# Smaller blocks, DMA transposes from tile 8 on, and a new load order in a fused chunk-attention and gated-FFN kernel

## The chip, the cores and the metric

One core of one Trainium2 chip runs the whole program. The metric is device time in microseconds (us), lower is better. The kernel before takes 240.97 us, the median of three runs that lie between 240.74 and 241.13.

## The reference

Chunked attention with memory tokens feeds a gated feed-forward network. There are 4 batches, 8 heads, 768 positions and 64 values per head. Each chunk of 32 queries sees 16 positions to its left, itself, 8 positions to its right, and 8 memory tokens.

```python
for c in range(S // 32):
    l_start, r_end = max(0, 32*c - 16), min(S, 32*c + 32 + 8)
    k_full = concatenate([mem_k, k[:, :, l_start:r_end]], axis=2)
    v_full = concatenate([mem_v, v[:, :, l_start:r_end]], axis=2)
    s = q[:, :, 32*c:32*c+32] @ k_full.T / sqrt(64)
    a = exp(s - max(s)); a = a / (sum(a) + 1e-9)
    out[:, :, 32*c:32*c+32] = a @ v_full
x = out.transpose(0, 2, 1, 3).reshape(3072, 512)
y = (relu(x @ w_gate) * (x @ w_val)) @ w_out       # 512 -> 1536 -> 512
```

Inputs and output are float32.

## The kernel before

**Tiles and blocks.** The 3072 token rows are cut into 24 tiles of 128 rows, 6 to a batch. Attention works tile by tile; the feed-forward network works on blocks of 2 or 4 consecutive tiles (`BLOCKS`, line 51). In a block, each of 12 hidden slices `m` takes four gate matmuls (`g_ps`) and four value matmuls (`v_ps`), both at line 408, as wide as the block (256 or 512 columns). ScalarE (ACT) applies the ReLU (line 414), VectorE (DVE) multiplies the two (line 420). Then each tile of the block takes 12 matmuls of 512 columns against `w_out` (line 433, `out_ps`), ACT copies the result out of PSUM and issues the store.

**Attention of one tile `a`.** Keys and queries are loaded by GpSimd's software DMA queue (POOL, `load_qk`, line 257) with a cast to bf16. Both have to be transposed. For tiles 6 to 10 TensorE (PE) does it (`qk_t`, line 279, 4 matmuls for k and 4 for q, then two copies out of PSUM). From tile `LATE_QK = 11` on, one transposing DMA issued by SyncE (SP) does both (`qk_transfer`, line 283); only the k half is then copied into `kT` (`qk_copy`). Tiles 0 to 5 come in pairs through line 238. The scores are line 310 on PE, followed by max, subtract, sum, reciprocal and normalise on DVE and the exponent on ACT. The probabilities P are transposed on PE for tiles below `LATE_P = 10` (line 359, 4 matmuls and a copy) and by a transposing DMA on SP from then on (line 363). The product with the values is line 389 (`xT_ps`, 16 matmuls; lines 375 and 382 for batch 0), and its copy into the block's `xT` starts the feed-forward matmuls of that block once all its tiles are there.

**Values.** For batches 1 to 3 the value rows are loaded by POOL straight into a zeroed block-diagonal tile `v_bd` (line 184, two large transfers `vl` and two small ones `ve` per batch). The upper context rows are then shifted into place by copies on ACT and DVE (`upper`, called `up` below; 8 for the first half of a batch's tiles and 8 for the second). The rows of the memory tokens (`mem_rows`, line 167, 8 transfers, called `mr`) go through SP for batch 1 and through POOL for batches 2 and 3.

**What sets the order.** Nothing is reordered on the chip: each engine runs its instructions in program order, waiting where an input is missing. The program order comes from a planner in the kernel (`schedule()`), which walks through time with estimated durations and lets each engine take the ready operation of best priority. Attention comes ahead of feed-forward matmuls, which fill what is left of PE. POOL's loads do not go through priorities; they are issued in the order in which they are listed, at most 8 in flight. The planner's estimates for a DMA's landing (`queue_end`, `LAND`, `LAND_P`) decide how far behind a transfer its users are placed in the order.

```python
late = [(a, i) for a in range(TPB, NT) for i in (1, 0)]     # k, q of tiles 6..23
...
for a, i in late[:5]: load_qk_op(a, i)                      # tiles 6, 7 and k of 8
for i in range(2): load(("wo", i), ...)                     # w_out
for b in range(1, B): ...                                   # values, memory rows, q and k by batch
```

Names used below: `vl 1` are the two big value transfers of batch 1, `t8` is the transposing transfer of tile 8's q and k, `pc8` that of its P.

Of the kernel before, what the change touches and what calls it, by code (L numbers as in the profile page):

```python
# [19 lines left out]
def kernel(  # L20
# [27 lines left out]
    KW = CH + NMEM  # L48
    CTX = 16 + CH + 8
    NSET = 2  # L50
    BLOCKS = [2, 2, 2, 4, 4, 4, 4, 2]
    GROUPS = [(0, 2), (2, 6), (6, 9), (9, 12)]
    BAND0 = 48
    UT = 3

    LATE_QK, LATE_P = 11, 10

    KEY_RUNS = ((0, CH, 0), (KW, 64, CH), (CH, KW, CTX))
    assert sum(BLOCKS) == NT and NMEM == 8 and D == 64 and H == 8
# [455 lines left out]


    ISSUE, SLACK = 1.5, 1.0
    LAND = {a: 4.0 if a < 16 else 3.5 if a < 19 else 2.0 for a in range(NT)}
    LAND_P = {a: 3.0 if a < 14 else 2.5 if a < 18 else 2.0 for a in range(NT)}

    def pace_t(a):
        return [("s", a - 5)]
# [136 lines left out]
    load_v_nat(5)  # L659
    for par in range(2):  # L660
        load(("vm", par), 256, 0.3, lambda par=par: mem_values(par))
    for a, i in late[:5]:
        load_qk_op(a, i)
    for i in range(2):
        load(("wo", i), 768, 4.1, lambda i=i: load_out(i))
    for b in range(1, B):
        deps = ([("z0", hp, c0) for hp in range(HP) for c0 in range(0, NCH, 8)] if b > 1 else [("z1", hp) for hp in range(HP)]) + ([("v", TPB * (b - NSET + 1) - 1)] + ['hold'] if b > NSET else [])
        if b == 1:
            for n in range(2 * HP):
                op(("mr", b, n), {"SP": 0.72}, lambda e, b=b, n=n: mem_rows(nc.sync, b, n),  # L670
                   deps + [(("vm", 0), 0.2), (("vm", 1), 0.2)], (0,))
        for par in range(2):
            load_v_op(b, par, deps)
        if b == 2:
            for n in range(2 * HP):
                load(("mr", 2, n), 192, 0.22, lambda n=n: mem_rows(nc.gpsimd, 2, n),
                     deps + [(("vm", 0), 0.2), (("vm", 1), 0.2)])
        for a, i in late[(5, 20, 26)[b - 1]:(20, 26, 36)[b - 1]]:
            load_qk_op(a, i)
    for n in range(2 * HP):  # L680
        load(("mr", 3, n), 192, 0.22, lambda n=n: mem_rows(nc.gpsimd, 3, n),
             deps + [(("vm", 0), 0.2), (("vm", 1), 0.2)])

    op("hold", {"DVE": 0.1}, lambda e: nc.vector.memset(v_bd[1][0:2 * CH, 0, 0, :].bitcast(F32), 0.0), [("v", 2 * TPB - 1)],  # L684
       prio=(0,), after=[("tc",17,1)])
# [6 lines left out]
    def schedule():  # L692
        done, started, times = {}, set(), [0.7]
        free = {e: 0.7 for e in ("PE", "ACT", "DVE", "SP", "POOL")}
        queue_end, flying, gives = 0.0, [], [(WARM + 0.15, "fps")]
        room["fps"] -= 1
        heapq.heappush(times, WARM + 0.15)
        todo = {e: [] for e in free}
        order, n_load = [], 0
        names = lambda o: [d[0] if timed(d) else d for d in o["deps"]] + o["after"]  # L700
        missing = {k: len(set(names(o))) for k, o in ops.items()}
        users = {}
        for k, o in ops.items():
            for d in set(names(o)):
                users.setdefault(d, []).append(k)

        def offer(k):
            for e in ops[k]["eng"]:
                bisect.insort(todo[e], (ops[k]["prio"], k), key=lambda x: x[0])

        for k in ops:
            if not missing[k]:
                offer(k)

        def ready(o, t, margin=0.0):
            if any(d not in started for d in o["after"]):
                return False
            for d in o["deps"]:
                d, lag = d if timed(d) else (d, 0.0)
                if d not in done or done[d] + lag + margin > t + 1e-9:  # L720
                    return False
            return all(room[r] >= o["take"].count(r) for r in o["take"])

        while len(started) < len(ops) + len(loads):
            t = heapq.heappop(times)
            while times and times[0] <= t + 1e-9:
                heapq.heappop(times)
            for g in [g for g in gives if g[0] <= t + 1e-9]:
                gives.remove(g)
                room[g[1]] += 1  # L730
            flying = [f for f in flying if f > t]
            moved = True
            while moved:
                moved = False
                for e in ("POOL", "PE", "ACT", "DVE", "SP"):
                    if free[e] > t + 1e-9:
                        continue
                    if e == "POOL":
                        if n_load == len(loads):
                            continue  # L740
                        o = loads[n_load]
                        if len(flying) >= 8 or not ready(o, t):
                            continue
                        n_load += 1
                        key = o["key"]
                        if o["n"]:
                            end = t + 0.62 + 0.27e-3 * o["n"]
                            queue_end = max(queue_end, end + 0.8) + o["work"]
                            flying.append(queue_end + 1.0)
                            done[key] = queue_end + (1.2 if n_load < 8 else 4.5 if key[:2] == ("vl", 1) else 2.4 if n_load < 45 else 6.0 if key[0] == "vl" else 4.0)  # L750
                        else:
                            end = done[key] = t + max(o["work"], 0.6)
                        fn = o["fn"]
                    else:
                        o = None
                        soon = False
                        for _, key in todo[e]:
                            late_pe = e == "PE" and t > 36.0 and ops[key]["prio"][0] == 1
                            if ready(ops[key], t, MARGIN if late_pe else 0.0):
                                o = None if soon and key[0] in ("up", "z0") else ops[key]  # L760
                                break
                            soon = soon or ready(ops[key], t + 0.3)
                        if o is None:
                            if e == "PE" and 1.3 < t < WARM:
                                order.append((t, lambda: idle_product(256)))
                                free[e] = t + (0.213 if t < 9.0 else 0.11)
                                heapq.heappush(times, free[e])
                            elif e == "PE" and t <= 1.3:
                                heapq.heappush(times, 1.31)
                            continue  # L770
                        for x in o["eng"]:
                            todo[x].remove((o["prio"], key))
                        d = o["eng"][e]
                        d, lat = d if isinstance(d, tuple) else (d, d)
                        d *= (1.8 if e == "PE" and t < 8.0 and key[0] in ("t", "p", "sh", "f") else 1.0)
                        end = t + d
                        done[key] = end + 0.25 if e == "PE" else t + lat + 0.08

                        if e == "SP" and key[0] in ("t", "pc"):
                            queue_end = max(queue_end, t + 1.5) + {"t": 2.6, "pc": 1.3}[key[0]]  # L780
                            done[key] = queue_end + 1.0
                        elif queue_end > t and key[0] == "oc":
                            queue_end += 0.7
                        fn = lambda o=o, e=e: o["fn"](e)
                        for g in o["give"]:
                            g, lag = g if isinstance(g, tuple) else (g, 0.0)
                            gives.append((done[key] + lag, g))
                            heapq.heappush(times, done[key] + lag)
                    for r in o["take"]:
                        room[r] -= 1  # L790
                    started.add(key)
                    for k in users.get(key, ()):
                        missing[k] -= 1
                        if not missing[k]:
                            offer(k)
                    order.append((t, fn))
                    free[e] = end
                    lags = {d[1] for k in users.get(key, ()) for d in ops[k]["deps"] if timed(d) and d[0] == key}
                    for x in [end] + [done[key] + lag + m for lag in lags | {0.0, 0.2, 1.5} for m in (0.0, MARGIN)]:
                        heapq.heappush(times, x)  # L800
                    moved = True
            assert times, [k for k in ops if k not in started][:20]
        return order
# [33 lines left out]
```

## Time and profile before

| | |
|---|---|
| median of three runs | 240.97 us |
| the profiled execution's own time | 240.65 us |
| its span, first to last instruction | 238.9 us (1.75 us lie around it) |
| granted TensorE clock | 0.998 |
| PE busy | 232.5 us, 97% of the span |
| DVE / ACT / POOL busy | 145.3 / 135.5 / 77.4 us |
| DMA moved | 26.88 MB, mean 113 GB/s |
| software DMA queue q0 (POOL) | 76128 packets, 14.65 MB |
| hardware DMA queue q1 (SP: transposes, memory rows) | 23312 packets, 5.53 MB |
| transposing transfers | 13 of q and k, 14 of P |

In the views, PE is the matmul side of TensorE and PEld its weight loads; a busy span of one matmul (about 380 ns at 512 columns) overlaps the next, so the pace is read from the starts of neighbouring groups. "L408" is line 408 of the kernel. Idle time is given in brackets with what ended it.

### The profile page before, as it was taken

How to read it: one execution, taken by the hardware profiler on the slowest of the kernel's cores; microseconds unless marked ns; L12 is line 12 of the kernel's file. 1: busy time of each engine (PE TensorE's matmuls, PEld its weight loads, DVE VectorE, ACT ScalarE, POOL GpSimd, SP SyncE). 2: the span in 40 equal slices, each digit the busy share in tenths (PEclk: the TensorE clock that was granted, in tenths of full speed). 3: DMA queues.
4: the chain of work that ended last, by engine and by line, in shares of the span. 5: the costliest groups of instructions: out<-in, count | busy, mean ns of one | idle time of the engine just before them, and what ended most of it. 6: DMA issues, size and time to landing. Idle time of an engine off the chain costs nothing.

```text
span 238.9 us, 6437 instructions
## 1 busy us (share of the span) xinstructions
PE 232.5 (97%) x2654; PEld 137.7 (58%) x2654; DVE 145.3 (61%) x292; ACT 135.5 (57%) x284; POOL 77.4 (32%) x102
## 2 busy tenths in 40 slices
PE   7898999999999999999999999999999999999994
PEld 5577887785589644455544444444555444445873
DVE  6674876987888389994279851599960043410430
ACT  7577777866885456897566851365523233312422
POOL 8975779313920374700094552100000000000000
PEclk9999999999999999999999999999999999999999
DMA  6999999999999999996199999995121300012102
GB/s 74 171 179 202 201 166 161 206 133 125 190 166 138 131 156 118 122 129 136 70 141 101 135 154 91 113 209 64 27 43 47 127 4 0 0 47 88 44 3 88
DMA packets 103069, 26.88 MB, mean 113 GB/s; under 512 B 94080, under 2 KB 99968, under 8 KB 103040
## 3 DMA queue, kind: packets, MB, share of 16 engines
q0 software_dynamic: 76128, 14.65, 92.7%
q1 hardware_dynamic: 23312, 5.53, 23.2%
q10 hardware_dynamic: 3600, 6.29, 8.4%
q8 instruction: 21, 0.34, 0.7%
q14 instruction: 8, 0.07, 0.2%
HBM read 28.55 MB, written 6.29 MB: 146 GB/s over the span
## 4 chain that ended last, share of the span: by engine, by line
PE 93%; DMA 2%; POOL 2%; issue 1%; ACT 1%; ACTq 0%; POOLq 0%
PE v_ps L408 27%; PE g_ps L408 26%; PE out_ps L433 26%; PE xT_ps L389 3%; PE s_ps L310 2%; DMA v_n<-in_v_dram 2%; PE idle_ps L140 2%; PE vs_ps L216 2%; PE xT_ps L382 2%; PE qk_ps L279 1%; PE pT_ps L359 1%; POOL qk_p L229 1%; PE qk_ps L238 1%; PE xT_ps L375 1%; POOL v_n L200 0%
## 5 line engine op out<-in xcount | busy, mean ns | idle before, releaser
L420 DVE TENSOR_TENSOR gvT<-v_ps,g_relu 128x256 f16<-128x256 f32 (+1 forms) x96 | 53.0, 554 | 48.7 <-PE v_ps L408 35.1
L408 PE MATMUL v_ps<-xT,w_val_sb 128*128 128x256 f16 (+1 forms) x384 | 78.2, 326 | 0.1
L408 PE MATMUL g_ps<-xT,w_gate_sb 128*128 128x256 f16 (+1 forms) x384 | 78.1, 326 | 0.0
L414 ACT ACTIVATE g_relu<-g_ps 128x256 f16<-128x256 f32 (+1 forms) x96 | 47.0, 490 | 41.5 <-PE g_ps L408 39.8
L433 PE MATMUL out_ps<-w_out_sb,gvT 128*128 128x512 f16 (+2 forms) x300 | 65.8, 371 | 0.0
L408 PEld LDWEIGHTS <-w_gate_sb 128*128 128x128 f16 x384 | 36.9, 98 | 24.8
L408 PEld LDWEIGHTS <-w_val_sb 128*128 128x128 f16 x384 | 35.9, 98 | 22.5 <-issue 0.5
L433 PEld LDWEIGHTS <-gvT 128*128 128x128 f16 x300 | 27.6, 97 | 29.5
L79 ACT COPY o_sb<-out_ps 128x512 f32<-128x512 f32 (+2 forms) x25 | 14.2, 568 | 29.6 <-PE out_ps L433 19.4
L323 DVE TENSOR_REDUCE mx<-s_ps 128x8 f32<-128x512 f32 x24 | 16.4, 685 | 13.9 <-PE s_ps L310 13.5
L338 ACT ACTIVATE p_exp<-dif 128x256 f16<-128x256 f32 (+2 forms) x72 | 19.6, 339 | 6.3 <-DVE dif L330 6.1
L184 POOL DMA_DIRECT2D v_bd<-in_v_dram x12 | 11.0, 924 | 33.6 <-DVE v_bd L684 19.2
L342 DVE TENSOR_REDUCE sm<-p_exp 128x8 f32<-128x512 f16 x24 | 16.4, 683 | 5.0 <-ACT p_exp L338 4.8
L257 POOL DMA_DIRECT2D qk_b<-in_k_dram x18 | 16.2, 902 | 9.7 <-DMA v_bd<-in_v_dram 5.4
L257 POOL DMA_DIRECT2D qk_b<-in_q_dram x18 | 16.2, 899 | 9.7 <-DMA v_bd<-in_v_dram 7.2
L79 ACT COPY v_bd<-v_bd 24x768 f16<-24x768 f16 (+1 forms) x23 | 18.5, 823 | 1.2 <-ACT o_sb L79 0.9
L353 DVE TENSOR_TENSOR p_n<-p_exp,rinv 128x512 f16<-128x512 f16 x24 | 16.5, 686 | 0.3
L330 DVE TENSOR_TENSOR dif<-s_ps,mx 128x512 f32<-128x512 f32 x24 | 16.2, 674 | 0.2
L79 ACT CAST xT<-xT_ps 128x512 f16<-128x512 f32 x17 | 10.0, 586 | 8.5 <-PE xT_ps L389 7.3
L167 POOL DMA_DIRECT2D v_bd<-vmem x16 | 10.2, 645 | 12.4 <-DMA qk_b<-in_q_dram 6.1
L140 PE MATMUL idle_ps<-idle 128*128 128x256 bf16 x69 | 11.3, 314 | 1.1 <-DVE warm L477 1.1
L389 PEld LDWEIGHTS <-v_bd 128*128 128x128 f16 x288 | 9.8, 96 | 3.6
(60 smaller groups left out, 165.6 us busy)
## 6 DMA issues: line engine op xcount, KB each, us to landing
out_dram<-o_sb ACTq DMA_DIRECT2D x23, 256.0 KB
qk_b<-in_k_dram POOLq DMA_DIRECT2D x18, 128.0 KB, 8.0
qk_b<-in_q_dram POOLq DMA_DIRECT2D x18, 128.0 KB, 8.9
v_bd<-in_v_dram POOLq DMA_DIRECT2D x6, 384.0 KB, 11.2
w_out_sb<-in_moe_w_out_dram POOLq DMA_DIRECT2D x2, 768.0 KB, 10.5
qk_p<-in_k_dram POOLq DMA_DIRECT2D x3, 256.0 KB, 5.3
qk_p<-in_q_dram POOLq DMA_DIRECT2D x3, 256.0 KB, 6.3
v_n<-in_v_dram POOLq DMA_DIRECT2D x6, 128.0 KB, 6.5
```

Source lines behind the costliest of these rows:

```text
L79: nc.scalar.copy(o, i)
L257: nc.gpsimd.dma_start(qk_b[a][:, 1 - i], bass.AP(tensor=x.tensor, offset=x[b, 0, 128 * t, 0].offset, ap=[[D, 128], [S * D, H], [1, D]]))
L323: nc.vector.reduce_max(SM[a, "mx"], s4, axis=AX.X)
L330: nc.vector.tensor_tensor(out=SM[a, "dif"].rearrange("p (m r) a s -> p r m a s", r=2), in0=S_ps.pop(a).rearrange("p r (m a) s -> p r m a s ...
L338: nc.scalar.activation(p[:, :, :, s0:s0 + k1 - k0], dif[:, :, :, k0:k1], ACT.Exp, scale=SCALE)
L342: nc.vector.reduce_sum(SM[a, "sm"], SM[a, "p"], axis=AX.X)
L353: nc.vector.tensor_tensor(out=P_n[a], in0=SM.pop((a, "p")), in1=rinv_b, op=ALU.mult)
L389: nc.tensor.matmul(ps[:, hp, r], lhsT=v_bd[b % NSET][:, hp, 4 * t + g, :], rhs=x[:, hp, r], start=True, stop=True)
L408: nc.tensor.matmul(ps, lhsT=w[:, f, 128 * m:128 * m + 128], rhs=xTs[blk][:, f, :], start=(f == 0), stop=(f == NFC - 1))
L414: nc.scalar.activation(st["r", m], st.pop((0, m)), ACT.Relu)
L420: nc.vector.tensor_tensor(out=st["gv"][:, m, :], in0=st.pop((1, m)), in1=st.pop(("r", m)), op=ALU.mult)
L433: nc.tensor.matmul(st["o", t, c], lhsT=st["gv"][:, m, 128 * t:128 * t + 128], rhs=w_out_sb[:, m, c[0]:c[1]], start=(m == 0), stop=(m == ND ...
```

## The change

- `BLOCKS` becomes 2, 2, 2, 2, 2, 4, 4, 4, 2: the first block of four (tiles 6 to 9) is cut in two, the rest keep their tiles.
- `LATE_QK` goes from 11 to 8 and `LATE_P` from 10 to 8: q and k of tiles 8, 9 and 10, and P of tiles 8 and 9, are transposed by DMA instead of on PE.
- POOL's list is written as `ORDER`: q and k of tiles 6 to 9 (8 loads), both halves of w_out, the values of batch 1, 10 loads (tiles 10 to 14), values and memory rows of batch 2, 8 loads (tiles 15 to 18), values of batch 3, 10 loads (tiles 19 to 23), memory rows of batch 3. Before, 5 loads stood ahead of w_out, 15 behind the values of batch 1 (to tile 15), and 6 behind batch 2.
- The planner's estimates change: landing margins of 3.0 (q, k) and 2.5 (P) for every tile, smaller margins for late loads, and a model in which transposing transfers run one after the other and each delays the software queue. These move instructions in the program order; they do no work themselves.

```diff
-    BLOCKS = [2, 2, 2, 4, 4, 4, 4, 2]
+    BLOCKS = [2,2,2,2,2,4,4,4,2]
...
-
-    LATE_QK, LATE_P = 11, 10
+    ORDER = [8, 'w0', 'w1', 'v1', 10, 'v2', 'm2', 8, 'v3', 10, 'm3']
+
+    LATE_QK, LATE_P = 8, 8
...
-    LAND = {a: 4.0 if a < 16 else 3.5 if a < 19 else 2.0 for a in range(NT)}
-    LAND_P = {a: 3.0 if a < 14 else 2.5 if a < 18 else 2.0 for a in range(NT)}
+    LAND = {a: 3.0 for a in range(NT)}
+    LAND_P = {a: 2.5 for a in range(NT)}
...
+    def v_deps(b):
+        z = [("z0", hp, c0) for hp in range(HP) for c0 in range(0, NCH, 8)] if b > 1 else [("z1", hp) for hp in range(HP)]
+        return z + ([("v", TPB * (b - NSET + 1) - 1), "hold"] if b > NSET else [])
...
+    n_qk = 0
+    for step in ORDER:
+        if isinstance(step, int):
+            for a, i in late[n_qk:n_qk + step]:
+                load_qk_op(a, i)
+            n_qk += step
+            continue
+        kind, b = step[0], int(step[1])
+        if kind == "w":
+            load(("wo", b), 768, 4.1, lambda b=b: load_out(b))
+        elif kind == "v":
+            for par in range(2):
+                load_v_op(b, par, v_deps(b))
+        else:
             for n in range(2 * HP):
...
+                load(("mr", b, n), 192, 0.22, lambda b=b, n=n: mem_rows(nc.gpsimd, b, n), mem_deps(b))
+    if "m1" not in ORDER:
+        for n in range(2 * HP):
+            op(("mr", 1, n), {"SP": 0.72}, lambda e, n=n: mem_rows(nc.sync, 1, n), mem_deps(1), (0,))
...
-                            done[key] = queue_end + (1.2 if n_load < 8 else 4.5 if key[:2] == ("vl", 1) else 2.4 if n_load < 45 else 6.0 if key[0] == "vl" else 4.0)
+                            done[key] = queue_end + (1.2 if n_load < 8 else 4.5 if key[:2] == ("vl", 1) else 2.4 if n_load < 45 else 3.5 if key[0] == "vl" else 2.5)
...
-                            queue_end = max(queue_end, t + 1.5) + {"t": 2.6, "pc": 1.3}[key[0]]
-                            done[key] = queue_end + 1.0
+                            double = key[0] == "t"
+                            busy = queue_end > t + 1.2
+                            begin = max(t + 1.2 + (3.0 if busy else 0.2), turn)
+                            if queue_end > begin:
+                                turn = begin + (3.8 if double else 2.7)
+                                queue_end += 1.6 if double else 0.9
+                            else:
+                                turn = begin + (1.5 if double else 0.9)
+                            done[key] = turn + 0.3
```

More of the change, by code (lines that the diff above doesn't have):

```diff
@@ L661, with mem_deps @@
         load(("vm", par), 256, 0.3, lambda par=par: mem_values(par))
[L662 to L668, printed above, removed]
-            for n in range(2 * HP):
[L670 to L682, printed above, removed]
+    def v_deps(b):
+        z = [("z0", hp, c0) for hp in range(HP) for c0 in range(0, NCH, 8)] if b > 1 else [("z1", hp) for hp in range(HP)]
+        return z + ([("v", TPB * (b - NSET + 1) - 1), "hold"] if b > NSET else [])
+    def mem_deps(b):
+        return v_deps(b) + [(("vm", 0), 0.2), (("vm", 1), 0.2)]
+    n_qk = 0
[12 more added lines that the diff above has]
+        else:
+            for n in range(2 * HP):
+                load(("mr", b, n), 192, 0.22, lambda b=b, n=n: mem_rows(nc.gpsimd, b, n), mem_deps(b))
+    if "m1" not in ORDER:
+        for n in range(2 * HP):
+            op(("mr", 1, n), {"SP": 0.72}, lambda e, n=n: mem_rows(nc.sync, 1, n), mem_deps(1), (0,))
     op("hold", {"DVE": 0.1}, lambda e: nc.vector.memset(v_bd[1][0:2 * CH, 0, 0, :].bitcast(F32), 0.0), [("v", 2 * TPB - 1)],
@@ L694, in schedule @@
         free = {e: 0.7 for e in ("PE", "ACT", "DVE", "SP", "POOL")}
-        queue_end, flying, gives = 0.0, [], [(WARM + 0.15, "fps")]
+        queue_end, turn, flying, gives = 0.0, 0.0, [], [(WARM + 0.15, "fps")]
         room["fps"] -= 1
```

## The prediction

> **What bounds the kernel now.** I read the page's busy line and its chain first.
>
> ```profile
> PE 232.5 (97%) x2654; PEld 137.7 (58%) x2654; DVE 145.3 (61%) x292; ACT 135.5 (57%) x284; POOL 77.4 (32%) x102
> PE 93%; DMA 2%; POOL 2%; issue 1%; ACT 1%; ACTq 0%; POOLq 0%
> ```
>
> PE sets the time: the chain that ended last runs on it for 93% of the span, and the view of waits gives PE 3.0 us of idle time in all, none of it after 50 us. So only two things can move the time: work taken from or given to PE, and waits that appear where none are now. The price of PE work comes from its timeline, from start to start, because busy spans overlap.
>
> ```profile
> 60.73 0.61 PE L279 MATMUL qk_ps<-ident_b,qk_b 128*128 128x128 bf16 x8
> 61.18 1.46 PE L433 MATMUL out_ps<-w_out_sb,gvT 128*128 128x512 f16 x6
> ...
> 68.56 0.38 PE L359 MATMUL pT_ps<-band,p_n 128*128 128x128 f16 x4
> 68.78 0.60 PE L408 MATMUL v_ps<-xT,w_val_sb 128*128 128x256 f16 x4
> 69.22 0.60 PE L408 MATMUL g_ps<-xT,w_gate_sb 128*128 128x256 f16 x4
> ...
> 157.77 1.03 PE L408 MATMUL g_ps<-xT,w_gate_sb 128*128 128x512 f16 x4
> 158.63 1.03 PE L408 MATMUL v_ps<-xT,w_val_sb 128*128 128x512 f16 x4
> ```
>
> Eight transposes of q, k cost 0.45 us, four of P 0.22, a group of four 256-wide matmuls 0.44, of four 512-wide ones 0.86.
>
> Then the waits that are close to becoming PE's. DVE's timeline near 60 us, and the landing of the second big value transfer of batch 1 (issued at 39.3, its row's maximum is its own):
>
> ```profile
> 58.80 1.30 DVE L81 COPY v_bd<-v_bd 24x768 f16<-24x768 f16 x3 [1.03 <-DMA v_bd<-in_v_dram]
> ...
> 63.79 0.69 DVE L342 TENSOR_REDUCE sm<-p_exp 128x8 f32<-128x512 f16 x1
> 64.39 0.68 DVE L323 TENSOR_REDUCE mx<-s_ps 128x8 f32<-128x512 f32 x1
> 64.99 0.19 DVE L346 RECIPROCAL rinv<-sm 128x8 f32<-128x8 f32 x1
> 65.11 0.69 DVE L330 TENSOR_TENSOR dif<-s_ps,mx 128x512 f32<-128x512 f32 x1
> 65.72 0.68 DVE L353 TENSOR_TENSOR p_n<-p_exp,rinv 128x512 f16<-128x512 f16 x1
> ```
> ```profile
> DMA to landing us min/median/max: 15.0/17.2/19.5
> ```
>
> DVE already waits for this landing (58.78) today; PE does not, because tile 6's value matmuls stand at 62.47. Late in the kernel ACT waits for the transposing transfer of tile 23's q, k, and PE uses it 1.5 us later:
>
> ```profile
> 162.75 0.62 ACT L79 COPY kT<-qk_T 128x512 bf16<-128x512 bf16 x1 [1.49 <-DMA qk_T<-qk_b]
> ```
> ```profile
> 164.25 0.31 PE L310 MATMUL s_ps<-kT,qk_T 64*32 64x64 bf16 x32
> 164.50 1.04 PE L408 MATMUL v_ps<-xT,w_val_sb 128*128 128x512 f16 x4
> 165.37 0.56 PE L389 MATMUL xT_ps<-pT,v_bd 128*128 128x32 f16 x16
> ```
>
> So DMA is the second bound, just behind PE, twice.
>
> **PE work.** The instruction order of the changed kernel has 24 transposes of q, k less (tiles 8 to 10) and 8 of P less. Saved: 3 x 0.45 + 2 x 0.23 = 1.81 us. Cutting tiles 6 to 9 into two blocks turns 24 groups of 512 columns into 48 of 256; with the medians over all groups, 0.863 and 0.437 us, that is 20.98 - 20.71 = 0.27 us more. Net **1.55 us less**, with no other place to go but the end, since PE never idles after 50 us. The chain's head (to 54 us) has the same PE order as before: no change.
>
> **Other engines.** The cut costs ACT 12 x (2 x 386 - 595) ns = 2.1 us and DVE 12 x (2 x 420 - 688) ns = 1.8 us; three q copies and two P copies out of PSUM fall away, some 3 x 0.6 + 2 x 0.5 = 2.8 us. Taken as nothing: between 76 and 80 us DVE is busy 2.39 and ACT 1.54 of 4.00 us. Without that room the 1.1 us left over would be added.
>
> **w_out moves behind three loads.** Three loads landed in 1.65 us (59.22 to 60.87) to 2.6 us (37.33 to 39.91). The second half of w_out landed at 48.7 and is first used at about 55.4, so it comes at 51.3 at the latest. Cost nothing; t8 (below) starts on its queue behind the memory rows, whose packets end at 51.5.
>
> **Values of batch 1, the first pinch.** Their last landing, 58.78, moves by those 1.65 to 2.6 us, and by t8 and t9, which are new here: SP issues them right behind the memory rows (46.4), beside these loads. What a transposing transfer takes from the software queue: while t11 to t14 ran, the last four loads landed between 69.13 and 80.37, 11.2 us for what needs 4 x 0.86 = 3.4, so 1.95 us each. Low end 1.4 (t19 with two P transfers, together its size again, cost nine loads 2.8 us: 133.5 to 144.4 instead of 9 x 0.9). High end 2.7: one P transfer, half as big, stretched the second value load of batch 3 to 6.9 us from 4.2 and 5.0 in batches 2 and 1. Two of them: 2.8 to 5.4, taken 3.9, as q, k transfers are the nearest row. Landing: 63.2 to 66.8, taken 58.78 + 2.1 + 3.9 = 64.8.
>
> A rule speaks on this. The Trainium skill ("DMA: Bandwidth & Descriptors", section "Queues, rings and completion order") says that each DMA engine takes turns between the queues it has work for, packet by packet; a transfer would then cost its neighbour its own packets only, and the row above speaks against that.
>
> What waits: DVE stands at the `up` copies, and behind them in its order are tile 7's sum and normalise, tile 8's max and subtract, tile 6's copy into xT and the next gate product. From landing: three copies 1.0, the five softmax steps 2.6 (63.79 to 66.40), xT 0.6, gate 0.45: 4.7 us. That gate frees the PSUM buffer for the fourth value group of block 2. Its place on PE: 54.1 + 48 x 0.216 (w_out) + 0.22 + 2 x 0.25 + 0.44 puts tile 6's values at 65.6; with their 0.42, four groups of 0.437 and P of tile 7 it is 68.0. Stall 64.8 + 4.7 - 68.0 = **1.5 us**, bounds 0 and 3.5.
>
> **Values of batch 2.** Issue to last landing was 12.0 us (81.35 to 93.32) with one P transfer issued near its end. Now pc9, pc10 and pc11 surround it, and t15 moves behind it with two loads more ahead of t16. One P transfer costs 0.7 to 2.7 us; PE's four PSUM buffers cover about 1.7. Taken 0.5, bounds 0 and 2.0.
>
> **Tile 18's values, the second pinch.** They stood at 165.37 behind tile 22's scores; the new order puts them ahead of these, after five 512-wide groups and two scores: 153.93 - 1.55 + 4.3 + 0.5 = 157.2. They need pc18, which SP issues behind t23. t23 waits for the buffer that tile 18's scores free; those move up three w_out groups, 1.95 + 1.55 = 3.5 us. pc18 landed at 163.1, so 159.6: a stall of 2.4 us, or nothing if the queue drains faster than before (memory rows are issued earlier). Taken **1.5**.
>
> **Sum** on the profiled execution's 240.65: -1.55 + 1.5 + 0.5 + 1.5 = +1.95, 242.6. The median lies 0.32 above that execution, so the prediction is 240.97 + 1.95 = **242.9 us**.
>
> **Rivals.**
> - *The cover holds* (faster). v1 lands at the low end, 63.2, and the later queues drain in time: stalls 0 to 1.0, so 239.4 to 240.5, likeliest 239.9. For it: the removed PE work is certain, and every margin above is within 2 us of holding. Against: the DVE row that waits today. It decides at a landing of about 64.0. Chance 0.28.
> - *Shared packet by packet* (no change). A q, k transfer alone ran its packets in 1.46 us (106.10 to 107.56); two delay v1 by 2.9: landing 63.8, stall 0.5; P transfers cost 0.9 and stay covered; 0.75 at tile 18. Sum -1.55 + 1.25: 240.7. With some friction up to 241.4. Against: 11.2 us for four loads. Chance 0.11. By the skill's rule of turns this would be the case.
> - *Each pinch at its bound* (much slower): 3.5 + 2.0 + 2.4 - 1.55 = +6.35, 247.3. For it: a late load delays the transfers that wait for it, and SP issues in order. Chance 0.12, from 245 up.
> - That the transposes are not gone is excluded by the order of the changed kernel.
>
> My forecast, 241.4 to 245, has 0.49; its own likely range is 241.5 to 244.5. A measurement of this kernel tells 0.2% (0.48 us) from no change, so faster 0.28, same 0.11, slower 0.61. The range 239.4 to 247.0 takes in the faster rival and most of the bad one.
>
> **What would show it.** In the profile after: PE's L279 group with x16 and L359 with x32; busy PE work shorter by about 1.5 us; DVE's `up` copies waiting for v_bd until 64 to 65, a gap on PE at line 408 or 389 near 66 to 70; gaps of PE near 157 to 160 at line 389. If v1 lands by 63.5 and PE shows no new idle time, I am wrong and the kernel gains 1 to 1.5 us.

## The result, and the profile after

The changed kernel takes **249.59 us**, the median of four runs (248.2 to 253.27), against 241.05 us of the kernel before on the same chip (240.74 to 241.8): a ratio of **1.033** (95% interval 1.0244 to 1.0417), some 8 us slower. The profiled execution took 250.94 us with a span of 249.2. Ratios here and below leave out executions in a disturbed state (one of the four here, one each of e3 and e4, two of e5), so a median and a ratio of the same kernel need not agree where few were undisturbed.

The page's busy line and the chain that ended last, of the changed kernel:

```profile
PE 234.3 (94%) x2718; PEld 145.2 (58%) x2718; DVE 144.6 (58%) x301; ACT 136.7 (55%) x294; POOL 77.7 (31%) x102
PE 64%; DMA 19%; ACT 5%; issue 4%; DVE 3%; POOL 2%; SPq 1%; ACTq 1%; POOLq 0%
```

PE was 93% of the chain and is 64%; DMA went from 2% to 19%, and the chain's line split gives `DMA qk_T<-qk_b` 14%: the transposing transfers of q and k. The transposes on PE are down to what the order of instructions promised (their two groups, from the view by line; line numbers have moved by one):

```profile
L360 PE MATMUL pT_ps<-band,p_n 128*128 128x128 f16 x32 | 3.1, 221 | 0.0
L280 PE MATMUL qk_ps<-ident_b,qk_b 128*128 128x128 bf16 x16 | 1.4, 220 | 0.0
```

**The first loss, 59 to 68 us.** ACT's timeline, then PE's, of the changed kernel (start, busy, operation, in brackets the idle time before it and what ended it):

```profile
61.35 0.62 ACT L80 COPY kT<-qk_T 128x512 bf16<-128x512 bf16 x1 [6.28 <-DMA qk_T<-qk_b]
...
62.02 0.30 PE L311 MATMUL s_ps<-kT,qT 64*32 64x64 bf16 x26 [3.03 <-ACT kT L80]
```

ACT stood 6.28 us at the copy of tile 8's keys, waiting for t8. Tile 7's scores need tile 8's first keys, so PE stood behind it for 3.03 us. The windows of PE (columns: window, its length, busy, granted clock, DMA share, GB/s):

```profile
59.00:62.00 3.00, 0.00 (x0) 1.00 2.27 106
62.00:65.00 3.00, 2.98 (x33) 0.57 3.04 135
65.00:68.00 3.00, 3.00 (x13) 0.87 2.39 190
```

After the idle stretch PE was granted 0.57 and 0.87 of its clock for 3 us each: 3 x 0.43 + 3 x 0.13 = 1.7 us more. (A window cut to the low clock, 62.40 to 65.80 us, shows 0.50.) The values of batch 1 also came late (issued at 42.6, the maximum is its own), but here that lay behind the wait for t8:

```profile
DMA to landing us min/median/max: 18.9/21.1/23.7
```

**The last loss, 161 to 169 us**, DVE, ACT and then PE of the changed kernel:

```profile
159.75 0.29 DVE L82 COPY kT<-qk_T 128x512 bf16<-128x512 bf16 x1 [1.67 <-DMA qk_T<-qk_b]
...
164.86 0.30 DVE L82 COPY kT<-qk_T 128x512 bf16<-128x512 bf16 x1 [2.65 <-DMA qk_T<-qk_b]
...
163.28 0.62 ACT L80 COPY kT<-qk_T 128x512 bf16<-128x512 bf16 x1 [4.90 <-DMA qk_T<-qk_b]
...
162.35 0.32 PE L311 MATMUL s_ps<-kT,qk_T 64*32 64x64 bf16 x32 [0.80 <-DVE dif L331]
165.14 1.02 PE L409 MATMUL v_ps<-xT,w_val_sb 128*128 128x512 f16 x4 [0.64 <-ACT o_sb L80]
168.35 0.32 PE L311 MATMUL s_ps<-kT,qk_T 64*32 64x64 bf16 x32 [1.18 <-DVE dif L331]
```

Again engines that run in order stand at key copies (159.75 is that of tile 21, 163.28 of tile 22, 164.86 of tile 23), and softmax steps, output copies and PSUM buffers are late behind them.

**A ledger.** The kernel computes a planned start for every PE instruction. Start in the trace minus planned start, and how much that delay grew in each stretch of the plan, in us:

| stretch of the plan | before | after | after, second trace (below) |
|---|---|---|---|
| to 50 us | 0.51 | 0.97 | 0.86 |
| 50 to 75 | -0.31 | 5.43 | 3.99 |
| 75 to 100 | -0.14 | -0.10 | 0.73 |
| 100 to 140 | -0.34 | 1.69 | 1.45 |
| 140 to 180 | -0.40 | 2.90 | 1.81 |
| plan's last PE start | 236.15 | 234.47 | 234.47 |
| last PE start in the trace | 235.54 | 245.49 | 243.44 |

The plan became 1.68 us shorter, and 11.6 us of delay against the plan ate that and 9.95 us more.

### The profile page after: what moved, and what is told of

Read it like the earlier page. It is cut to its first block, busy times and chain, and to the rows that moved or that the text cites. A ratio compares the mean times of both kernels' runs of the same rounds, so it can differ in the third digit from the quotient of the medians.

```text
span 249.2 us, 6615 instructions
## 1 busy us (share of the span) xinstructions
PE 234.3 (94%) x2718; PEld 145.2 (58%) x2718; DVE 144.6 (58%) x301; ACT 136.7 (55%) x294; POOL 77.7 (31%) x102
## 4 chain that ended last, share of the span: by engine, by line
PE 64%; DMA 19%; ACT 5%; issue 4%; DVE 3%; POOL 2%; SPq 1%; ACTq 1%; POOLq 0%
PE v_ps L409 19%; PE g_ps L409 19%; PE out_ps L434 16%; DMA qk_T<-qk_b 14%; DMA v_bd<-in_v_dram 4%; DMA v_n<-in_v_dram 2%; PE xT_ps L390 2%; PE idle_ps L141 2%; PE vs_ps L217 2%; PE s_ps L311 2%; ACT v_bd L80 1%; ACT o_sb L80 1%; ACT p_exp L339 1%; SPq L168 1%; PE xT_ps L383 1%
## 5 line engine op out<-in xcount | busy, mean ns | idle before, releaser
L421 DVE TENSOR_TENSOR gvT<-v_ps,g_relu 128x256 f16<-128x256 f32 (+1 forms) x108 | 54.3, 508 | 54.8 <-PE v_ps L409 37.4
L409 PE MATMUL v_ps<-xT,w_val_sb 128*128 128x256 f16 (+1 forms) x432 | 80.2, 308 | 1.0 <-ACT o_sb L80 0.6
L409 PE MATMUL g_ps<-xT,w_gate_sb 128*128 128x256 f16 (+1 forms) x432 | 80.2, 308 | 0.4 <-ACT g_relu L415 0.4
L415 ACT ACTIVATE g_relu<-g_ps 128x256 f16<-128x256 f32 (+1 forms) x108 | 48.5, 455 | 40.5 <-PE g_ps L409 38.5
L434 PE MATMUL out_ps<-w_out_sb,gvT 128*128 128x512 f16 (+2 forms) x300 | 67.3, 377 | 0.0
L409 PEld LDWEIGHTS <-w_gate_sb 128*128 128x128 f16 x432 | 41.2, 98 | 21.2 <-issue 1.0
L409 PEld LDWEIGHTS <-w_val_sb 128*128 128x128 f16 x432 | 40.8, 98 | 20.9 <-issue 2.2
L434 PEld LDWEIGHTS <-gvT 128*128 128x128 f16 x300 | 28.3, 99 | 31.0 <-issue 2.3
L80 ACT COPY v_bd<-v_bd 24x768 f16<-24x768 f16 (+1 forms) x26 | 20.9, 821 | 2.0 <-ACT o_sb L80 1.3
L258 POOL DMA_DIRECT2D qk_b<-in_k_dram x18 | 16.2, 902 | 16.7 <-DMA v_bd<-in_v_dram 12.9
L80 ACT COPY kT<-qk_T 128x512 bf16<-128x512 bf16 x10 | 6.2, 620 | 16.0 <-DMA qk_T<-qk_b 15.1
```

The costliest lines, as they stand in the source:

```text
L80: nc.scalar.copy(o, i)
L258: nc.gpsimd.dma_start(qk_b[a][:, 1 - i], bass.AP(tensor=x.tensor, offset=x[b, 0, 128 * t, 0].offset, ap=[[D, 128], [S * D, H], [1, D]]))
L409: nc.tensor.matmul(ps, lhsT=w[:, f, 128 * m:128 * m + 128], rhs=xTs[blk][:, f, :], start=(f == 0), stop=(f == NFC - 1))
L415: nc.scalar.activation(st["r", m], st.pop((0, m)), ACT.Relu)
L421: nc.vector.tensor_tensor(out=st["gv"][:, m, :], in0=st.pop((1, m)), in1=st.pop(("r", m)), op=ALU.mult)
L434: nc.tensor.matmul(st["o", t, c], lhsT=st["gv"][:, m, 128 * t:128 * t + 128], rhs=w_out_sb[:, m, c[0]:c[1]], start=(m == 0), stop=(m == ND ...
```

## The experiments

Theory A: the saved PE work is there, but transposing transfers land later than the places that the planner gives their users, and in-order engines stand at the key copies. Rivals: the later values of batch 1 (C, the prediction's own first pinch), the estimates alone (D), the new transfers alone (E), the small blocks (B), transfers that cannot be hidden under any plan (H).

### Each part alone, and the transfers undone

e1, blocks alone, on the kernel before:

```diff
-    BLOCKS = [2, 2, 2, 4, 4, 4, 4, 2]
+    BLOCKS = [2,2,2,2,2,4,4,4,2]
```

> The kernel before with the new block sizes alone (2, 2, 2, 2, 2, 4, 4, 4, 2); transposes, load order and estimates as before. Theory A (the time went to transposing transfers that land later than the places that the plan gives their users): tiles 8 to 10 are still transposed on PE, so nothing new waits; 24 groups of 256 columns more and 12 of 512 fewer than before cost PE 0.27 us: 241.2, between 240.7 and 241.8. Rival B (the small blocks themselves bring waits, since gates, sums and PSUM buffers turn over in smaller pieces): 243 or more, with a gap on PE between 60 and 90 us.

Measured 242.66 us, ratio 1.0052 (1.0028 to 1.0077): by the ratio 1.25 us slower than the 241.47 beside it. That is neither A's 0.2 nor B's 2 us. PE work explains 0.27; about 1 us more is lost in small waits, such as these of PE in e1:

```profile
67.84 0.38 PE L279 MATMUL qk_ps<-ident_b,qk_b 128*128 128x128 bf16 x4 [0.38 <-DMA qk_b<-in_q_dram]
106.83 0.60 PE L408 MATMUL g_ps<-xT,w_gate_sb 128*128 128x256 f16 x4 [0.20 <-ACT g_relu L414]
```

e2, the order of loads alone (old transfers, blocks and estimates):

```diff
+    ORDER = [8, 'w0', 'w1', 'v1', 10, 'v2', 'm2', 8, 'v3', 10, 'm3']
```

> The kernel before with the new order of loads alone (eight late q, k loads ahead of w_out instead of five, ten ahead of the values of batch 2 instead of fifteen). Theory A: no transposing transfer stands near 50 us here, so only the second value load of batch 1 lands later, by three loads of 0.6 to 0.9 us each: 61 instead of 58.8, which the prediction's own working leaves covered: 241.0, between 240.6 and 241.6. Rival C (the later values of batch 1 are what costs, as the prediction had it): 242 to 243.5, with a gap of PE near 66 to 70.

242.33 us, ratio 1.0038 (1.0015 to 1.0062), 0.9 us: more than A's "covered" and less than C, which had 1 us or more. The delay grew by 0.81 between 50 and 75 us where it fell by 0.31 before, in waits of 0.2 us of PE on ACT near 68 to 71 us.

e3, the estimates alone:

```diff
+    LAND = {a: 3.0 for a in range(NT)}
+    LAND_P = {a: 2.5 for a in range(NT)}
+    ... (the queue's model and margins as in the change)
```

> The kernel before with the planner's new landing estimates alone (3.0 us for every transposing transfer of q, k, 2.5 for P, and shorter times for the load queue); no work is moved between engines. Theory A (the first cause is tile 8's transfer at 48 to 61 us, which this kernel does not have): up to 80 us as before, and later only the part of the loss that tiles 15 to 23 had, 1 to 3 us: 242 to 244. Rival D (the estimates cause all of it: the plan places users too early everywhere): 247 to 250. Rival E (the estimates are harmless, the new transfers alone cost): within 0.5 us of 241.

244.64 us, ratio 1.0114 (1.0052 to 1.0176), 2.7 us: as A said, against D and E. No work moved between engines; PE's largest new wait is again a key copy that ACT could not do, of tile 20:

```profile
145.69 0.62 ACT L79 COPY kT<-qk_T 128x512 bf16<-128x512 bf16 x1 [4.38 <-DMA qk_T<-qk_b]
...
146.36 0.29 PE L310 MATMUL s_ps<-kT,qk_T 64*32 64x64 bf16 x26 [1.73 <-ACT kT L79]
```

e4, the changed kernel with the transfers put back:

```diff
-    LATE_QK, LATE_P = 8, 8
+    LATE_QK, LATE_P = 11, 10
```

> The changed kernel with the transposing transfers back at tile 11 for q, k and tile 10 for P; blocks, order of loads and estimates stay new. Theory A: the gap of 3.0 us at 59 to 62 and the low granted clock behind it are gone (tile 8 is transposed on PE); 1.55 us plus some of PE work come back, and the losses of tiles 15 to 23 stay: 244 to 247. Rival D (estimates): as slow as the changed kernel, 248 or more. Rival E (only the new transfers of tiles 8 to 10 cost): 241 to 242.

Ratio 1.0139 (1.0058 to 1.0221), 3.4 us over before with an interval of 1.4 to 5.3, in A's range: the earlier transfers cost the rest of the 8 us. The three parts without them, 1.25 + 0.9 + 2.7, would add up to 4.9, which lies inside this interval, so whether they overlap is not shown.

### The same work, other places in the order

e5, users of t8 and t9 placed later; no other line is edited, though the planner places what follows anew:

```diff
-    LAND = {a: 3.0 for a in range(NT)}
+    LAND = {a: 9.0 if a in (8, 9) else 3.0 for a in range(NT)}
```

> The changed kernel, with the planner told that the transposing transfers of tiles 8 and 9 land 9.0 us after their turn instead of 3.0: the same transfers, copies and matmuls, only tile 8's key copy and tile 7's scores stand later in the orders of ACT and PE. Theory A (ACT stood 6.3 us at tile 8's key copy, PE 3.0 us behind it, and the granted clock fell for 3.4 us after): gap and clock drop at 59 to 66 are gone or under 1 us, the losses of tiles 15 to 23 (some 4.5 us) stay: 245 to 247. Rival C (the values of batch 1 cost the time there): their last landing at 66.3 now shows as a gap of 2 us or more at line 409 near 66 to 70, and the kernel stays at 247 to 250. Rival F (the planned place does not matter, the clock falls by itself): 248 or more.

Ratio 1.0136 (1.0096 to 1.0175) from two executions, 244.5 us, 0.5 under A's range; the profiled execution took 244.02. In it the gap at 59 and the low clock are gone. But C was right in part: with t8 out of the way, the values of batch 1 show, though in several waits under 1 us and not in a total of 247 or more. DVE and PE of e5:

```profile
62.38 1.81 DVE L82 COPY v_bd<-v_bd 24x768 f16<-24x768 f16 x5 [6.11 <-DMA v_bd<-in_v_dram]
...
67.65 0.49 PE L390 MATMUL xT_ps<-pT,v_bd 128*128 128x32 f16 x12 [0.91 <-ACT v_bd L80]
69.71 0.60 PE L409 MATMUL v_ps<-xT,w_val_sb 128*128 128x256 f16 x4 [0.70 <-ACT o_sb L80]
```

The delay grew by 2.68 between 50 and 75 us: the prediction's first pinch, where it had put it. One expectation of A failed: the losses of the later tiles did not stay. From 100 to 140 us the delay fell by 0.34 and from 140 to 180 it grew by 0.28, against 1.69 and 2.90 in the changed kernel, although the estimates of tiles 19 to 23 were the same. So the late loss also depends on how late the kernel already runs, or on what the planner placed anew; which of the two is not shown.

e6, users of tiles 19 to 23 placed later:

```diff
+    LAND = {a: 7.0 if a >= 19 else 3.0 for a in range(NT)}
```

> The changed kernel, with the planner told that the transposing transfers of tiles 19 to 23 land 7.0 us after their turn instead of 3.0; tile 8 as in the changed kernel. Theory A: the gap of 3.0 us at 59 to 62 stays, that at 161 to 169 (3.3 us over tiles 20 to 22) goes, with less than 1 us left of it: 244.5 to 247. Rival G (the late transfers of tiles 19 to 23 are only pushed later, the waits go to the values and the end): 248 or more, with PE gaps at line 390 behind 165 us.

Ratio 1.0168 (1.0136 to 1.0200), 245.3 us, as A said, and the delay behind 140 us fell by 0.39 as in the kernel before; G is out. PE in e6 where 161 to 169 us was the loss (columns: window, its length, then busy of PE, PEld, DVE, ACT, POOL, clock, DMA share, GB/s):

```profile
155.00:160.00 5.00, 5.00 (x69) 2.47 (x68) 2.44 (x5) 1.17 (x2) 0.00 (x0) 1.00 0.88 216
160.00:165.00 5.00, 5.00 (x56) 2.20 (x54) 3.95 (x8) 3.57 (x9) 0.00 (x0) 1.00 0.29 82
165.00:170.00 5.00, 5.00 (x86) 2.17 (x85) 4.67 (x9) 3.52 (x10) 0.00 (x0) 1.00 0.11 23
```

One expectation failed: no gap of 3 us at 59 to 62. SP came to t8 at 43.1 instead of 48.4, it landed at 58.2, and the loss up to 75 us was 3.52 in another form.

e7, the changed kernel with an estimate for each tile, for q, k (below) and for P (1.0 to 6.9), and later ones for the values, chosen against the landings of the traces of before and after (so e7 has the blocks, transfers, load order and PE work of the changed kernel):

```diff
+    LAND = {..., 8: 4.0, 9: 5.9, 10: 4.6, 11: 3.0, 12: 2.9, 13: 5.7, 14: 8.1, 15: 3.0, 16: 3.5, 17: 6.7, 18: 6.4, 19: 12.3, 20: 6.2, 21: 11.3, 22: 11.9, 23: 5.5}
-    ... 4.5 if key[:2] == ("vl", 1) else 2.4 if n_load < 45 else 3.5 if key[0] == "vl" else 2.5)
+    ... 8.9 if key[:2] == ("vl", 1) else 2.4 if n_load < 45 else 6.4 if key[0] == "vl" else 1.7)
```

> The changed kernel with the same blocks, order of loads and transfers from tile 8, but a landing estimate for each tile (4.0, 5.9, 4.6, 3.0, 2.9, 5.7, 8.1, 3.0, 3.5, 6.7, 6.4, 12.3, 6.2, 11.3, 11.9, 5.5 us for q, k of tiles 8 to 23; 1.0 to 6.9 for P) and later ones for the values. It issues exactly the PE work of the changed kernel. Theory A (all of the loss is lateness against the plan): nearly all of the 8 us come back, 240.5 to 243. Rival H (transfers from tile 8 on cannot be hidden, whatever the plan): 245 or more. If the saved 1.55 us of PE work shows in full, 239.5 to 240.

242.71 us, ratio **1.0061** (1.0043 to 1.0080): of the 8 us, 6.5 come back with the same work. Its chain, and PE's largest wait behind 50 us:

```profile
PE 91%; ACT 2%; DMA 2%; POOL 2%; issue 1%; DVE 0%; ACTq 0%; DVEq 0%; POOLq 0%
```
```profile
PE v_ps L409 <- ACT g_relu L415: 0.8, 2, 0.7
```

That settles A against H, with A taken widely: the users of the late values were moved as well. The delay grows by 0.37 between 50 and 75 us and by 1.21 between 100 and 140, where ReLUs and `up` copies share ACT with 256-wide groups. Against before these are 0.7 and 1.55 more, with 0.3 at the start 2.5 in all, above the 1.55 us of saved PE work.

e8, the same from tile 9 on (other estimates for each tile):

```diff
+    LATE_QK, LATE_P = 9, 9
```

> As the last one, but transposing transfers of q, k and P from tile 9 on (tile 8 is transposed on PE, 0.7 us more of PE work), with estimates of its own for each tile. Theory A (tile 8's transfer, beside the memory rows, w_out and the first loads, is the worst placed of all): 239.5 to 242, not slower than the last one in spite of the added PE work. Rival H: 245 or more.

241.96 us, ratio 1.0023 (1.0012 to 1.0033): faster than e7 by 0.4% in spite of 0.7 us more PE work. Tile 8's transfers do not seem worth what they save; the estimates differ too, so this is not shown apart.

### The changed kernel again, and pauses of PE

e9 is the changed kernel itself.

> The changed kernel itself, once more, for a second trace. Theory A2 (refined by the runs so far: in the changed kernel's trace SP came to tile 8's transfer at 48.4 us and it landed at 61.3; with the same place in the order it was issued at 43.1 and landed at 58.2 in the run with later users of tiles 19 to 23): either the transfer lands behind 60 again and PE idles about 3 us at 59 to 62 (total about 251), or it lands near 58, PE does not idle there, and the late values of batch 1 (landing near 66) cost 2.5 to 3.6 us at 65 to 75 instead (total about 248). Theory A as first put (tile 8's transfer is the main loss in every execution): a gap of 3 us at 59 to 62 in any case.

Measured 248.07 us (two executions), ratio 1.0278 (1.0227 to 1.0330). The profiled execution took 248.89 us. t8 was issued at 43.8 and landed at 59.5. PE of this second trace:

```profile
56.72 0.81 PE L434 MATMUL out_ps<-w_out_sb,gvT 128*128 128x512 f16 x3 [0.80 <-DMA w_out_sb<-in_moe_w_out_dram]
60.18 0.29 PE L311 MATMUL s_ps<-kT,qT 64*32 64x64 bf16 x26 [0.34 <-ACT kT L80]
68.44 0.36 PE L390 MATMUL xT_ps<-pT,v_bd 128*128 128x32 f16 x8 [0.41 <-ACT v_bd L80]
70.70 0.60 PE L409 MATMUL v_ps<-xT,w_val_sb 128*128 128x256 f16 x4 [1.01 <-ACT o_sb L80]
```

e9 shows A2's second branch: t8 costs 0.4 us of delay here, the late w_out 1.0, and the stretch from 65 to 75 us, where the values of batch 1 are late, 2.4. The theory as first put, a gap of 3 us in any execution, is false: t8 and the values share one stretch, and whichever is later sets the loss, 4.0 us here and 5.4 with the low clock in the first trace.

e10 puts two pauses into the kernel before:

```diff
+    gaps = [(188.0, 0, 16), (206.0, 1, 44)]
+    def pause(b, n):        # PE reads a dead buffer, GpSimd clears it, PE reads it again
+        ...
+        nc.gpsimd.memset(g.bitcast(F32), 0.0)
```

> The kernel before with two pauses of PE put in where only the last blocks are left: behind a small matmul GpSimd clears a dead buffer and PE reads it again, once with 1024 words per partition near 188 us, once with 2816 near 206; at about 1 ns a word (224 halves took 0.32 us) and some 0.4 us of hand-over, gaps of about 1.4 and 3.2 us. If a gap of about 3 us lowers the clock that PE is granted and one of about 1.4 does not (as the gaps of 3.0 and 1.2 us in the changed kernel suggest): PEclk 1.00 behind the first, about 0.5 for some 3.4 us behind the second, total 241 + 4.6 + 1.7 = 247.5. If the low clock behind 62 us had another cause (transfers in flight): PEclk 1.00 behind both, total 245.5.

The pauses on PE, and the windows of e10 (columns as for e6):

```profile
189.07 0.23 PE L812 MATMUL s_ps<-v_bd 128*128 128x128 f16 x1 [1.13 <-POOL v_bd L811]
210.53 0.23 PE L812 MATMUL s_ps<-v_bd 128*128 128x128 f16 x1 [2.61 <-POOL v_bd L811]
```
```profile
190.00:193.00 3.00, 3.00 (x15) 1.36 (x14) 0.57 (x1) 1.18 (x2) 0.00 (x0) 1.00 0.25 93
211.00:214.00 3.00, 3.00 (x10) 1.16 (x9) 0.65 (x1) 0.60 (x1) 0.00 (x0) 0.60 0.00 0
214.00:217.00 3.00, 3.00 (x13) 1.23 (x12) 0.73 (x2) 0.60 (x1) 0.00 (x0) 0.83 0.00 0
```

Measured 247.43 us, ratio 1.0252 (1.0211 to 1.0293). That the total meets the expected 247.5 is partly luck, as the pauses came out 0.9 us shorter in all than expected. Full clock behind the pause of 1.13 us; 0.60 and 0.83 behind that of 2.61, with no DMA traffic at all: 3 x 0.40 + 3 x 0.17 = 1.7 us, as in the changed kernel. The idle stretch itself lowers the clock.

### Is there a better kernel?

e11 starts the q, k transfers later and keeps four blocks of 4 (with the new order of loads, and estimates for each tile); e12 stays nearest to the kernel before:

```diff
e11:
+    BLOCKS = [2,2,4,2,4,4,4,2]
+    LATE_QK, LATE_P = 10, 8
e12:
+    BLOCKS = [2,2,4,2,4,4,4,2]
+    LATE_QK, LATE_P = 10, 10
```

> What the theory would build: blocks of 2, 2, 4, 2, 4, 4, 4, 2 tiles (as many of 4 as before), transposing transfers of P from tile 8 but of q, k from tile 10 only, the new order of loads, and a landing estimate for each tile. PE work 0.45 + 2 x 0.23 = 0.91 us below the kernel before. Theory A2 (what counts is that no user is planned ahead of its landing): 240.0 to 241.3. Rival H (transfers from tile 8 on cannot be hidden): over 243. Rival B (block sizes bring waits of their own): 241.5 to 242.5.

> The kernel before with blocks of 2, 2, 4, 2, 4, 4, 4, 2 tiles, transposing transfers of q, k and P from tile 10 (q, k of one tile more), the old order of loads and the old estimate of the queue, with a landing estimate for each tile. PE work 0.45 us below. Theory A2: 240.4 to 241.3. Rival B: 241.5 to 242.5.

241.43 us, ratio 1.0008 (0.9995 to 1.0022), and 241.45 us, ratio 1.0012 (0.9998 to 1.0027), against 241.03. Neither differs measurably from the kernel before: 0.9 and 0.45 us of saved PE work are used up by new small waits (e11's delay grows by 0.61 between 100 and 140 us, where it fell by 0.34 before). Both times lie between A2's ranges, which end at 241.3, and B's, which begin at 241.5, so they do not settle what the block sizes cost. No version was found that beats the kernel before.

## Why the prediction was wrong in size

The sign was right (slower), with DMA as the second bound that gives back more than PE saves. The size was not: 242.9 with a range to 247.0, against 249.59.

- **PE work, right.** x16 and x32 as said, and the plan became shorter by 1.68 us, against 1.55. Busy PE time, which was expected to fall by 1.5 as a sign of it, rose all the same, from 232.5 to 234.3 us and to 233.1 in the second trace; the low clock of the first trace is part of that, the rest was not traced.
- **Other engines "taken as nothing", mis-sized.** e1 shows 1 us beyond the 0.27 of PE, close to the 1.1 us that the text named as the price without cover. That ACT and DVE cause all of it is not shown: the longest wait there, 0.38 us, was for a load of queries.
- **"w_out comes at 51.3 at the latest. Cost nothing", wrong.** It landed at 52.64 and, in the second trace, at 56.67, where PE waited 0.80 us.
- **The step that failed: "t8 starts on its queue behind the memory rows".** The working priced t8, and the q, k transfers of the other tiles, only as neighbours of other loads, never as transfers that somebody waits for. The user of t8, the key copy, stood at 55.07 on ACT, and t8 landed at 61.33 (58.0 to 59.5 in e5, e6, e7 and e9). Up to 3.0 us of idle PE, and the 1.7 us of low clock behind it, are in no term and in no rival. What the runs showed in its place: the loss sits at users that are placed ahead of the landings, and e7 brings back 6.5 of the 8 us by moving these alone.
- **The gap is not the whole of it.** In the second trace t8 cost only 0.4 us, and that execution still took 6.0 us more than forecast. There the excess is spread: the late w_out 1.0, the first pinch 0.9 over its price of 1.5, 75 to 100 us 0.9 against before, and the two later pinches 1.8 and 2.2 against before where 0.5 and 1.5 were taken. How much each would cost alone was not tested.
- **Values of batch 1: the mechanism right, the size at its bound.** Landing of the second big transfer, by what was added:

| kernel | landing, us | against before |
|---|---|---|
| before | 58.78 | |
| three loads ahead (e4) | 60.68 | +1.9 (taken 2.1) |
| and one q, k transfer beside it (e8) | 62.17 | +3.4 |
| and two of them (after, second trace, e5, e6, e7) | 65.5 to 66.3 | +6.8 to +7.6 |

Taken for the two transfers: 3.9, with bounds 2.8 and 5.4; measured 66.33 - 60.68 = 5.65 in the changed kernel, 4.9 at least. The two cost over three times as much as the one in e8 (1.5). By the rule of turns in the Trainium skill ("DMA: Bandwidth & Descriptors", section "Queues, rings and completion order") the pair would cost, as an estimate, its own packets, 2 x 1.46 = 2.9; the one transfer agrees with that, the pair does not. By e2, which has the same three loads ahead and where the small transfer right behind this one landed 0.4 us later than in e4, both prices would be 0.4 lower, and the pair's still 4.4 or more. Why the pair costs so much more stays open. The stall, taken 1.5 with a bound of 3.5, was 2.4 (second trace) to 2.7 (e5, whole stretch); no run moved these values alone, so this share is read from the traces.
- **Values of batch 2: 0.5, bound 2.0.** The delay grew by 1.69 and 1.45 between 100 and 140 us, 2.0 and 1.8 against before. The transfer itself took no longer (11.0 us from 93.11 to 104.11, against 12.0); it was issued later, short groups met busy ACT and DVE, and two waits of 0.22 and 0.36 us at 123 and 129 us stand behind a key copy and a softmax step.
- **The second pinch: right stretch, wrong transfer.** 1.5 us at tile 18's values was forecast, and PE has no gap there; 3.3 us against before were lost (2.2 in the second trace), at the key copies of tiles 21 to 23, and e6 takes the loss away by moving these users.
- **The estimates** were described as moving instructions; the working gave them no price. Alone they cost 2.7 us (e3), and correcting them brings back 6.5 (e7).
- **Rivals.** "Each pinch at its bound", 247.3 us, came nearest, partly by luck: t8's gap, the low clock and the late w_out are not in it, and its last pinch lay at other transfers. "The cover holds" and "packet by packet" are out: v1 landed 2.3 us after the 64.0 at which the first decides, and later still after the 68.0 - 4.7 = 63.3 that the working's own sum gives for that point.

## What to carry to other kernels

Where work moves from an engine to DMA, cost each new transfer twice: for what it takes from its neighbours, and for the first in-order engine that stands at its result. Where a planner sets the order, its landing estimates are part of the work: here the same instructions in another order took 249.6 or 242.7 us. And where TensorE sets the time, add to a long stall (2.6 us was long enough here, 1.7 was not) what its clock loses behind it.

## What the runs showed of the hardware

- Idle stretches of PE of 2.61 us (e10) and 3.03 us (the changed kernel) were each followed by a granted clock of 0.50 over 3.40 us (211.58 to 214.98 and 62.40 to 65.80), which began 1.05 and 0.38 us after PE had started again; 1.7 us were lost each time. Behind stretches of 1.13 us (e10), 1.18 us (the changed kernel) and 1.73 us (e3) the clock stayed at 1.00. The Trainium skill ("TensorE: Matmul & The Clock Gate", section "HAM oscillation — how this bites in real kernels") warns of idle gaps above about 3.4 us; here 2.61 us was enough.
- The time of a transposing transfer of 256 KB depends on what else is in flight: issue to landing 3.1 us for tile 14 of the changed kernel (85.61 to 88.67), 12.9 for tile 8 (48.44 to 61.33), beside w_out, the values and the memory rows. Its issue alone held SP for 4.4 us there and 7.0 in e6.
